# Three subtractions of a gated-mix kernel moved from VectorE to GpSimd, and ScalarE's copies moved behind the value rows

## The chip, the cores and the metric

The kernel runs on one core of a Trainium2 chip. TensorE (PE) multiplies, VectorE (DVE), ScalarE (ACT) and GpSimd (POOL) work element by element, and SyncE (SP) issues the DMAs. Each engine takes its instructions in the order in which the program lists them; semaphores make an instruction wait for another engine. The metric is the device time of one execution in microseconds (us), lower is better.

## The reference

For 2048 tokens of 576 features, the result mixes an attention with a compressive memory (32 heads of 18, four segments of 512 tokens) and a GEGLU feed-forward layer of 4608 hidden features:

```python
x = A_x                                              # (1, 2048, 576)
g = _sigmoid((x * gate_w).sum(-1, keepdims=True))
a = _A_ref(x, wq, wk, wv, wo, beta)                  # segments s = 0..3, memory M, z
b = (_gelu(x @ w_gate) * (x @ w_up)) @ w_down
return g * a + (1 - g) * b

# in _A_ref, for each segment s:
p = _softmax(qs @ ks.T * scale + mask);  a_dot = p @ vs
a_mem = (phi(qs) @ M) / (phi(qs) @ z + 1e-6)
o = g * a_mem + (1 - g) * a_dot
M = M + phi(ks).T @ vs;  z = z + phi(ks).sum()
```

## The kernel before

All float32 operands are split into a high and a low float16 word, and a product is the sum of three products of words. The program first projects x to queries, keys and values, one segment of 512 tokens at a time (s = 0 to 3, the first 212 us), and then runs 72 steps of the feed-forward layer with attention heads placed between the products.

The order of the instructions on each engine is that in which the code is written (a manual schedule); no planner reorders them.

A segment s from 1 to 3 begins with four rows of values, q = 0 to 3, of 128 tokens each. In one row, TensorE forms the first half of the values (`vrows(s, q, 0)`), turns the keys of the segment before (`key_rows`, bank G and V), forms the second half (`vrows(s, q, 1)`), reads the memory with the queries (`recall`, two banks "st", line 683), and adds the row of the segment before to the memory (`memorize`, line 737). For these, VectorE writes the low words of the values (`vstage`, line 654) and of the keys (`krow`, line 724), and normalises what was recalled (`put_recall`: lines 694 to 705, of which line 703 multiplies two 128x32 tensors in SBUF and line 705 reads the banks "st" for the last time). A bank of PSUM can be written again only when these have read it. After the rows come nine projections (`project`, line 447).

The feed-forward products are formed by a scheme with fewer products that needs sums of quarters of x. `load_sums(p)` brings two segments into `acc`; `form_sums(p, i, half, by)` makes the i-th of three sums (line 482, a float32 subtraction of 128x1024, both inputs in SBUF), its high word on ScalarE (line 484) and its low word on VectorE (line 486, again two inputs in SBUF); `last_sum` makes the fourth (its subtraction, line 491, always ran on GpSimd). For p = 0 this lies in the rows of s = 2, for p = 1 the subtractions lie in the rows of s = 3 and the words in its projections.

GpSimd otherwise sets the last column of a `vstage` buffer at each row's beginning (line 647, a memset that waits until `memorize` has let go of an older buffer). In s = 3 it scales the first weights (`scales_out`, lines 275 to 278, then `scale_g`, line 303).

Of the kernel before, what the change touches and what calls it, by code (L numbers as in the profile page):

```python
# [45 lines left out]
def kernel(ctx: ExitStack, tc: tile.TileContext, xs, wqk, wv, wo, wgu, wd, beta, out):  # L46
    nc = tc.nc
    pe, act, dve, pool, sp = nc.tensor, nc.scalar, nc.vector, nc.gpsimd, nc.sync
# [19 lines left out]
    def flat(ap):  # L68
        return ap.rearrange("p a b -> p (a b)") if len(ap.shape) == 3 else ap
# [102 lines left out]
    def add_squares(c, ks, to=0, by=pool):  # L172

        for k in ks:
            a, b = (x_sq[c][:, i * L : (i + 1) * L] for i in (to, k))
            by.tensor_tensor(a, a, b, OP.add)
# [42 lines left out]
    def rescale(c):  # L219

        a, b = slice(c, c + 1), slice(c + 1, c + 2)
        v = rescales[c] = cst.tile([P, 1], F32, name="xr", tag="xr", bufs=2)
        dve.tensor_scalar(v, xsc[:, b], xis[:, a], None, OP.mult)
        for t in (xsc, xis):
            dve.tensor_copy(t[:, a], t[:, b])

    def rescale_words(c):
        dve.tensor_scalar(flat(x16[c]), flat(x16[c]), rescales.pop(c), None, OP.mult)
# [235 lines left out]
    def load_sums(p):  # L464
        c = 2 * p
        r = sums_x[p] = {}
        o = (1 + 4 * p) * 2 * L
        for i in range(2):
            for h in range(2):
                r[h + 1, i + 1] = kept["words"][:, o + 2 * h * L : o + 2 * (h + 1) * L]  # L470
            sp.dma_start(kept["words"][:, o : o + 4 * L], flat(xs[c + i, :, 0:4]))
            o += 4 * L

    def form_sums(p, i, half, by=dve):

        r, sc = sums_x[p], xsc[:, 2 * p : 2 * p + 1]
        t = kept["xt"][p] if half >= 0 else None
        k, o, a, b = ((0, (1, 1), (1, 2), (1, 1)), (2, (1, 2), (2, 2), (1, 2)), (1, (2, 2), (2, 2), (1, 1)))[i]
        if t is not None:
            hi, lo = (flat(t[:, 4 * k + j : 4 * k + j + 2]) for j in (0, 2))  # L480
        if half <= 0:
            by.tensor_tensor(r[o], r[a], r[b], OP.subtract)
        if half == 0 or half == 2:
            act.activation(hi, r[o], AF.Copy, scale=sc)
        if half == 1:
            dve.scalar_tensor_tensor(lo, r[o], sc, hi, OP.mult, OP.subtract)
# [39 lines left out]
    with tc.tile_pool(name="prj", bufs=2, side="right", reuse_waits="tile") as pp:  # L526
# [56 lines left out]
        def finish_later():  # L583
            while later:
                later.pop(0)()
# [55 lines left out]
        def put_rows(s, q, b, pv, unit, a):  # L641

            hf, c = divmod(s, 2)
            t = 4 * c + q
            if b == 0:
                st = vst[s, q] = pa.tile([P, H, VC], F16, name="vstage", bufs=6)
                pool.memset(st[:, :, VC - 1 : VC], 1.0)
            st = vst[s, q]
            p3 = pv[:, :NH].rearrange("p (h d) -> p h d", d=DH)
            hs = slice(16 * b, 16 * b + 16)  # L650
            act.activation(st[:, hs, DH : 2 * DH], p3, AF.Copy, scale=unit)

            def rest():
                dve.scalar_tensor_tensor(st[:, hs, 0:DH], p3, unit, st[:, hs, DH : 2 * DH], OP.mult, OP.subtract)
                if b:
                    dve.tensor_scalar(gate[:, 0, 8 * hf + t : 8 * hf + t + 1], pv[:, NH : NH + 1], a, None, OP.mult)
                    sp.dma_start(vps[hf][t * P : (t + 1) * P, :], flat(st))

            later.append(rest)
# [117 lines left out]
        with tc.manual_schedule(engines=ORDERED):  # L777
# [91 lines left out]
            def beside_rows(s, q):  # L869
                if 0 < s < 3 and q == 0:  # L870
                    add_squares(s, range(1, KT))
                if s == 1 and q == 1:
                    add_squares(0, range(1, KT))
                if s == 1 and q == 0:
                    load_sums(0)
                if s == 1 and q == 2:
                    rescale(0)
                    rescale_words(0)
                if s == 2:
                    if q > 1:  # L880
                        form_sums(0, q - 2, 1)
                    if q:
                        form_sums(0, q - 1, 0)
                if s == 3 and q == 0:
                    rescale(2)
                    for i in range(2):
                        squares(0, 1, i, lambda o, r: square_sum(o, r, True))
            def behind_rows(s, q):
                if s == 3:
                    if q == 1:  # L890
                        scales(0)
                        scales_out(0)
                        scale_g(0)
                        scale_g(1)
                    if q < 3:
                        form_sums(1, q, -1, pool if q == 0 else dve)
                    if q == 3:
                        rescale_words(2)
                        high_g(0, 0)
                        low_g(0, 0)  # L900
# [91 lines left out]
            for s in range(4):  # L992
                p = s - 1
                if s:
                    for q in range(4):
                        pv = vrows(s, q, 0)
                        if q == 0:
                            key_scale(p)
                        if done:
                            put_columns(*done)  # L1000
                            done = None
                        finish_later()
                        put_rows(s, q, 0, *pv)
                        if s == 3 and q == 0:
                            norm_x(3, bank("V"))
                        if q:
                            key_rows(p, q - 1)
                        beside_rows(s, q)
                        finish_later()
                        if held:  # L1010
                            held.pop()()
                        behind_rows(s, q)
                        pv = vrows(s, q, 1)
                        put_rows(s, q, 1, *pv)
                        if p >= 1:
                            recall(p, q)
                        if q:
                            memorize(p, q - 1)
                    finish_later()
                    key_rows(p, 3)  # L1020
                for j in range(9):
                    if j == 1 and s:
                        make_gate(s)
                    if s and j == 0:
                        memory_scale(p)
                    if s or j > 1:
                        pr = project(s, j)
                    elif j == 0:
                        prs = project_first()
                        pr = prs[0]  # L1030
                    else:
                        pr = prs[1]
                    if s and j == 0:
                        finish_later()
                        memorize(p, 3)
                    if s == 0 and j in (2, 3, 5, 6):
                        make_qk(j + 2 + (j == 3))
                    if done and (s, j) != (0, 1):
                        for d in done if isinstance(done, list) else [done]:
                            put_columns(*d)  # L1040
                    done = [done, pr] if (s, j) == (0, 1) else pr
                    if s and j == 1:
                        keep_memory(p)
                    if s == 3 and j == 1:

                        first.close()
                        mp2 = stay.enter_context(tc.tile_pool(name="ffn2", bufs=2, reuse_waits="tile"))
                        xt.append(mp2.tile([P, 12, L], F16, name="xt1", bufs=1))
                        home.update(r=mp2)
                    beside_products(s, j)  # L1050
                    finish_later()
                    if (s, j) == (1, 3):
                        make_gate(0)
                    if s == 0 and j >= 6:
                        q = j - 5
                        pv = vrows(0, q, 1)
                        put_rows(0, q, 1, *pv)
                    if s == 3 and j == 6:
                        recall(3, 0, (("dn", 2), ("dn", 2)))
                        recall(3, 1, (("V",), ("pv",)))  # L1060
                    if s == 3 and j == 7:
                        recall(3, 2, (("dn", 2), ("dn", 2)))
# [766 lines left out]
```

## Time and profile before

| | us |
|---|---|
| median of 3 runs | 1555.67 (1555.64 to 1556.55) |
| span of the profiled execution | 1553.8 |
| what lies around the span, by the median | 1.9 |
| PE busy | 1548.4 |
| POOL busy | 1305.8 |
| DVE busy | 1229.3 |
| ACT busy | 1183.7 |

No separate time is given for the profiled execution; the median is 1.9 us above its span, which is taken for what lies around it. Busy time of PE is that of pipelined matmuls with modelled ends, so it is read together with the waits. A segment's place in the span: the rows of s = 2 lie from 99 to 122 us, those of s = 3 from 151 to 175 us.

### The profile page before, as it was taken

The numbers are of one execution on the slowest core, as the hardware profiler recorded it, in microseconds if no ns is written. First come the engines' busy times: TensorE is split into PE (matmuls) and PEld (weight loads), VectorE is DVE, ScalarE is ACT, GpSimd is POOL, SyncE is SP. The second block draws the span as 40 slices with busy tenths as digits, with TensorE's granted clock in tenths as the row PEclk, the third lists the DMA queues.
The fourth block names the chain that finished last, engine by engine and source line by source line (L and its number), as shares of the span: only waits on it lengthen the run. The fifth ranks groups of instructions, "written<-read, shape, count | busy, mean of one in ns | idle before, by whom it ended". The sixth has DMA issues, their size and how long they took to land.

```text
span 1553.8 us, 33925 instructions
## 1 busy us (share of the span) xinstructions
PE 1548.4 (100%) x12195; PEld 955.7 (62%) x12196; DVE 1229.3 (79%) x3198; ACT 1183.7 (76%) x2037; POOL 1305.8 (84%) x1313
## 2 busy tenths in 40 slices
PE   9999999999999999999999999999999999999999
PEld 5665655666666566666666665666666666666577
DVE  6788976778878887878788887878787878887665
ACT  7567544888888888888888888888888888876421
POOL 3544778899898999989899989898999989899597
PEclk9999999999999999999999999999999999999999
DMA  7533341667768687778777878878687878774654
GB/s 254 195 127 125 132 150 34 122 126 140 133 131 141 130 144 130 144 126 137 132 136 126 140 139 136 135 140 151 127 138 133 144 128 141 130 136 99 120 118 138
DMA packets 472601, 210.14 MB, mean 135 GB/s; under 512 B 427632, under 2 KB 437360, under 8 KB 471920
## 3 DMA queue, kind: packets, MB, share of 16 engines
q1 hardware_dynamic: 472432, 207.97, 67.6%
q8 instruction: 96, 1.57, 0.4%
q14 instruction: 73, 0.60, 0.1%
HBM read 92.03 MB, written 27.26 MB: 77 GB/s over the span
## 4 chain that ended last, share of the span: by engine, by line
PE 94%; POOL 3%; ACT 2%; DVE 1%; issue 1%; POOLq 0%
PE dn L1228 27%; PE U L1268 22%; PE V L1268 12%; PE pv L1183 4%; PE G L385 3%; PE st L447 3%; PE dn L454 2%; PE U L1275 2%; PE dn L385 1%; PE U L447 1%; PE V L1280 1%; PE G L1280 1%; PE st L1137 1%; PE G L447 1%; PE st L1669 1%; PE V L1275 1%
## 5 line engine op out<-in xcount | busy, mean ns | idle before, releaser
L1228 PE MATMUL dn<-paird,hh 128*128 128x288 f16 x3396 | 476.5, 286 | 0.2
L1164 POOL TENSOR_TENSOR pf<-pf,ph 128x512 f16<-128x512 f32 (+1 forms) x256 | 359.2, 1403 | 94.6 <-ACT ph L1163 83.6
L1228 PEld LDWEIGHTS <-hh 128*128 128x128 f16 x3456 | 332.2, 98 | 139.1 <-issue 18.1
L1268 PEld LDWEIGHTS <-pairg 128*128 128x128 f16 x2616 | 244.0, 98 | 254.8 <-issue 18.3
L1236 DVE SCALAR_TENSOR_TENSOR acc<-dn,ev,acc 128x288 f32<-128x288 f32 x534 | 274.4, 515 | 51.4 <-PE dn L1228 42.9
L1153 ACT ACTIVATE pf<-pf,mb,esc 128x512 f32<-128x512 f32 (+3 forms) x512 | 293.0, 642 | 5.2
L1268 PE MATMUL U<-xt,pairg 128*128 128x512 f16 x864 | 209.9, 379 | 0.2 <-DVE gl L1459 0.2
L1268 PE MATMUL U<-x,pairg 128*128 128x512 f16 x840 | 204.1, 379 | 0.0
L426 POOL TENSOR_TENSOR pairg<-raw,pairg 128x640 f16<-128x640 f32 (+2 forms) x144 | 176.2, 1239 | 3.0 <-ACT pairg L418 1.5
L1163 ACT ACTIVATE ph<-pf 128x512 f16<-128x512 f32 (+1 forms) x256 | 172.4, 720 | 0.0
L1255 POOL TENSOR_TENSOR hh<-gl,hh 128x512 f16<-128x512 f32 x144 | 164.4, 1163 | 7.5 <-ACT hh L1254 7.5
L1140 DVE CUSTOM_DVE_ANT_0 pf<-st,mask 128x512 f32<-128x512 f32 (+1 forms) x256 | 157.2, 614 | 0.0
L418 ACT ACTIVATE pairg<-raw 128x640 f16<-128x640 f32 (+2 forms) x144 | 89.3, 647 | 56.6 <-POOL raw L410 36.2
L1258 ACT ACTIVATE gl<-gl,sc 128x512 f32<-128x512 f32 x144 | 97.2, 716 | 40.7 <-DVE gl L1505 30.1
L303 POOL TENSOR_SCALAR raw<-raw,sc 128x640 f32<-128x640 f32 x72 | 118.7, 1663 | 0.0
L1459 DVE COPY gl<-U 128x512 f32<-128x512 f32 x72 | 49.8, 692 | 85.4 <-PE U L1268 74.9
L1150 ACT ACTIVATE mb<-mx,esc 128x4 f32<-128x4 f32 x128 | 37.5, 293 | 103.4 <-DVE mx L1140 103.4
L1140 DVE CUSTOM_DVE_ANT_0 pf<-dn,mask 128x256 f32<-128x256 f32 (+1 forms) x192 | 67.2, 375 | 55.3 <-PE dn L1137 55.3
L1268 PE MATMUL V<-xt,pairg 128*128 128x512 f16 x432 | 105.7, 381 | 0.0
L1268 PE MATMUL V<-x,pairg 128*128 128x512 f16 x432 | 104.8, 378 | 0.0
L1254 ACT ACTIVATE hh<-gl 128x512 f16<-128x512 f32 x144 | 82.6, 616 | 16.0 <-DVE gl L1250 15.8
L1183 PEld LDWEIGHTS <-pt 128*128 128x128 f16 x2560 | 83.4, 96 | 12.3
(354 smaller groups left out, 2971.1 us busy)
## 6 DMA issues: line engine op xcount, KB each, us to landing
raw<-in_wgu_dram SPq DMA_DIRECT2D x36, 640.0 KB
rawd<-in_wd_dram SPq DMA_DIRECT2D x36, 288.0 KB
qk<-stage SPq DMA_DIRECT2D x36, 256.0 KB
qt<-qk SPq DMA_DIRECT2D x128, 72.0 KB
kt<-qk SPq DMA_DIRECT2D x128, 72.0 KB
vp<-vstage SPq DMA_DIRECT2D x16, 296.0 KB
vt<-vp SPq DMA_DIRECT2D x16, 296.0 KB
qt<-qk SPq DMA_DIRECT2D x128, 36.0 KB
```

What stands on the lines that cost most here:

```text
L303: pool.tensor_scalar(r, r, scl[f // 2][0][:, 0:1], None, OP.mult)
L426: pool.tensor_tensor(spot(f, *p, 1), raw_g[f][:, p[0] : p[1]], spot(f, *p, 0), OP.subtract)
L1140: dve.tensor_tensor_reduce(prob[a][:, COL[qi] : COL[qi] + (qi + 1) * P], out[qi], mask[:, L - (qi + 1) * P :], 1.0, -3e38, OP.add, OP.max, ...
L1153: act.activation(r, r, AF.Exp, bias=b[:, qi : qi + 1], scale=esc[:, 0, c : c + 1])
L1163: act.activation(h[:, cols], p[:, cols], AF.Copy)
L1164: pool.tensor_tensor(p.bitcast(F16)[:, cols], p[:, cols], h[:, cols], OP.subtract)
L1183: pe.matmul(ov, pr[:, 10 * i + COL[qi] // P + kb], v[:, 4 * e + kb, c0 : c0 + VC], start=kb == 0 and i == 0, stop=kb == qi and i == 1)
L1228: pe.matmul(o[:, :NH], hh[:, a, q * P : (q + 1) * P], w[:, b, n * NH : (n + 1) * NH], start=i == 0, stop=i == 5)
L1236: dve.scalar_tensor_tensor(av, o[:, :NH], ev, av, OP.mult, OP.add)
L1255: pool.tensor_tensor(hh[:, 1], t, hh[:, 0], OP.subtract)
L1258: act.activation(t, o, AF.Gelu_apprx_tanh, scale=scl[f // 2][0][:, 2 + c : 3 + c])
L1268: pe.matmul(o, w[:, i, (a + k) * P : (a + k + 1) * P], x[:, b + k], start=start and k == 0 and i == 0 and b == h, stop=k == 1 and i == 1, ...
```

## The change

In s = 2 the subtractions for i = 1 and i = 2 (rows q = 2 and q = 3) go from VectorE to GpSimd; that for i = 0 (row q = 1) stays on VectorE. The ScalarE copies (line 484) of all three go from before the row's second half to behind it. In s = 3 the subtraction for i = 1 (row q = 1) goes to GpSimd, ahead of `scales(0)`; it stood behind that on VectorE. That for i = 0 was on GpSimd and that for i = 2 stays on VectorE.

```diff
                     if q > 1:
                         form_sums(0, q - 2, 1)
                     if q:
-                        form_sums(0, q - 1, 0)
+                        form_sums(0, q - 1, -1, pool if q > 1 else dve)
...
                 if s == 3:
+                    if q < 2:
+                        form_sums(1, q, -1, pool)
                     if q == 1:
                         scales(0)
                         scales_out(0)
                         scale_g(0)
                         scale_g(1)
-                    if q < 3:
-                        form_sums(1, q, -1, pool if q == 0 else dve)
+                    if q == 2:
+                        form_sums(1, q, -1)
...
                         pv = vrows(s, q, 1)
                         put_rows(s, q, 1, *pv)
+                        if s == 2 and q:
+                            form_sums(0, q - 1, 2)
```

On GpSimd in the rows of s = 2 (the memsets are those of the rows q = 1, 2 and 3; line 176 sums squares of x, line 491 is `last_sum`, line 629 belongs to the projections):

```order
 L647 MEMSET vstage 128x32
 L176 TENSOR_TENSOR pairg_960<-pairg_960 128x512 x4
-L647 MEMSET vstage 128x32 x3
+L647 MEMSET vstage 128x32 x2
+L482 TENSOR_TENSOR acc<-acc 128x1024
+L647 MEMSET vstage 128x32
+L482 TENSOR_TENSOR acc<-acc 128x1024
 L491 TENSOR_TENSOR acc<-acc 128x1024
 L629 TENSOR_TENSOR phi<-phi,expm 128x512
```

One subtraction now follows the memset of row q = 2, one that of row q = 3, and `last_sum` follows the second directly.

On VectorE in row q = 3 of s = 2 (behind `put_recall` of the row before):

```order
 L705 TENSOR_TENSOR mo<-st,rden 128x180
 L486 SCALAR_TENSOR_TENSOR xt_102<-acc,xsc,xt_102 128x1024
-L482 TENSOR_TENSOR acc<-acc 128x1024
 L654 SCALAR_TENSOR_TENSOR vstage<-dn,vstage 128x16x18
 L724 SCALAR_TENSOR_TENSOR krow_173<-G,kmc,krow_173 128x448
```

The subtraction between the low word of the sum before and the values' low words is gone; the same piece stands in row q = 2.

On GpSimd in row q = 1 of s = 3 (the first subtraction is i = 0, the memset is that of row q = 1):

```order
 L482 TENSOR_TENSOR acc<-acc 128x1024
 L647 MEMSET vstage 128x32
+L482 TENSOR_TENSOR acc<-acc 128x1024
 L275 TENSOR_SCALAR sc<-v 128x2
 L276 TENSOR_SCALAR sc<-xis,v 128x4
```

The second subtraction stands directly behind the memset and ahead of the scales.

## Rows read from the trace of the kernel before

**Rows 1.** Page, part 1: busy us (share of span) xinstructions of each engine.

```profile
PE 1548.4 (100%) x12195; PEld 955.7 (62%) x12196; DVE 1229.3 (79%) x3198; ACT 1183.7 (76%) x2037; POOL 1305.8 (84%) x1313
```

**Rows 2.** Busy time by window: stretch, its us, each engine's busy us, clock, DMA.

```profile
98.00:125.00 27.00, 27.00 (x234) 22.43 (x233) 25.22 (x67) 11.86 (x23) 12.31 (x12) 1.00 0.40 138
150.00:176.00 26.00, 26.00 (x230) 22.08 (x229) 24.06 (x71) 12.74 (x30) 20.16 (x19) 1.00 0.49 165
```

**Rows 3.** Waits of PE from 98 to 250 us: total us, times, longest.

```profile
PE U L1268 <- DVE gl L1459: 0.2, 1, 0.2
```

**Rows 4.** Timeline, DVE, rows of s = 2: start, us, instruction, [idle before].

```profile
108.58 0.46 DVE L654 SCALAR_TENSOR_TENSOR vstage<-dn,vstage 128x288 f16<-128x288 f32 x1 [0.31 <-ACT vstage L651]
...
110.19 0.19 DVE L703 TENSOR_TENSOR rden<-rden,gh 128x32 f32<-128x32 f32 x1
...
113.48 0.45 DVE L654 SCALAR_TENSOR_TENSOR vstage<-dn,vstage 128x288 f16<-128x288 f32 x1
...
115.08 0.46 DVE L654 SCALAR_TENSOR_TENSOR vstage<-dn,vstage 128x288 f16<-128x288 f32 x1 [0.31 <-ACT vstage L651]
...
116.69 0.19 DVE L703 TENSOR_TENSOR rden<-rden,gh 128x32 f32<-128x32 f32 x1
...
119.98 0.45 DVE L654 SCALAR_TENSOR_TENSOR vstage<-dn,vstage 128x288 f16<-128x288 f32 x1
120.35 0.68 DVE L724 SCALAR_TENSOR_TENSOR krow<-G,kmc,krow 128x448 f16<-128x448 f32 x1
```

**Rows 5.** Timeline, POOL: memsets of s = 2, memset and subtraction of s = 3.

```profile
109.81 0.24 POOL L647 MEMSET vstage<- 128x32 f16 x1 [0.33 <-PE pv L737]
115.97 0.24 POOL L647 MEMSET vstage<- 128x32 f16 x1 [5.92 <-PE pv L737]
...
155.46 0.24 POOL L647 MEMSET vstage<- 128x32 f16 x1
155.54 2.35 POOL L482 TENSOR_TENSOR acc<-acc 128x1024 f32<-128x1024 f32 x1
```

**Rows 6.** Timeline: VectorE with two SBUF inputs beside a GpSimd tensor-tensor.

```profile
128.07 0.63 DVE L756 TENSOR_TENSOR bd<-bd,kjunk 128x456 f32<-128x456 f32 x1
...
172.04 3.47 POOL L426 TENSOR_TENSOR pairg<-raw,pairg 128x640 f16<-128x640 f32 x2 [0.69 <-ACT pairg L418]
...
174.89 0.67 DVE L703 TENSOR_TENSOR rden<-rden,gh 128x32 f32<-128x32 f32 x1
...
179.10 2.35 POOL L491 TENSOR_TENSOR acc<-acc 128x1024 f32<-128x1024 f32 x1
...
179.87 2.08 DVE L756 TENSOR_TENSOR bd<-bd,kjunk 128x456 f32<-128x456 f32 x1
...
185.28 1.27 POOL L629 TENSOR_TENSOR phi<-phi,expm 128x512 f32<-128x512 f32 x1 [0.90 <-DVE phi L628]
...
185.80 1.83 DVE L486 SCALAR_TENSOR_TENSOR xt<-acc,xsc,xt 128x1024 f16<-128x1024 f32 x1
```

**Rows 7.** Timeline: VectorE subtractions beside GpSimd instructions with one tensor input.

```profile
161.20 1.26 POOL L275 TENSOR_SCALAR sc<-v 128x2 f32<-128x2 f32 x1 [3.13 <-DVE v L268]
...
165.27 3.91 POOL L303 TENSOR_SCALAR raw<-raw,sc 128x640 f32<-128x640 f32 x2
...
166.22 1.22 DVE L482 TENSOR_TENSOR acc<-acc 128x1024 f32<-128x1024 f32 x1
```

**Rows 8.** Timeline, PE: recall and memorize in row q = 3 of s = 2.

```profile
119.73 1.37 PE L683 MATMUL st<-bd,phi 128*128 128x152 f32 x10
120.94 0.82 PE L737 MATMUL U<-vstage,krow 128*128 128x152 f16 x9
```

**Rows 9.** Timeline, row q = 1 of s = 3: DVE's normalising, PE's next recall.

```profile
158.22 0.19 DVE L703 TENSOR_TENSOR rden<-rden,gh 128x32 f32<-128x32 f32 x1
158.45 0.82 DVE L705 TENSOR_TENSOR mo<-st,rden 128x396 f32<-128x396 f32 x2
...
159.76 1.37 PE L683 MATMUL st<-bd,phi 128*128 128x152 f32 x10
```

## The prediction

> **What bounds the kernel now.** First the page: PE is busy for 1548.4 of 1553.8 us [rows 1]. Then the stretches in which the change lies: in the rows of s = 2 and of s = 3, PE and VectorE are both busy throughout (27.00 and 25.22 of 27 us, 26.00 and 24.06 of 26 us), while GpSimd has 12.31 and 20.16 us of work in them [rows 2]. Then PE's waits from 98 to 250 us: a single one, 0.2 us [rows 3]. So TensorE sets the time, and VectorE runs close behind it without holding it up. Work taken from VectorE shortens nothing here; whatever makes VectorE late by more than its slack becomes a wait of PE, and later work does not give it back, since PE is busy there too.
>
> How small the slack is, two places show. In row q = 3 of s = 2, `memorize` starts at 120.94 with nine products about 0.07 us apart [rows 8]; its third is the first to read the low words of the keys, at 121.08. VectorE writes these from 120.35 to 121.03 [rows 4]: 0.05 us to spare. In row q = 1 of s = 3, `recall` starts at 159.76 into the banks that line 705 has finished reading at 159.27 [rows 9]: 0.49 us to spare.
>
> **What is removed.** Three subtractions leave VectorE, 1.22 us each [rows 7], 3.66 us together. They stood behind work on which PE waits nowhere, so their removal is worth 0 to the time, at the very most the 0.2 us of [rows 3]. The three copies on ScalarE keep their number and size. Ahead of them now stands the copy of the values' second half, for which VectorE waited 0.31 us in row q = 2 and in the one after [rows 4]; these waits go. ScalarE has 11.86 us of work in 27 [rows 2], so the copies are hidden behind the values there; the low word that reads each copy comes a row later. If that cover were gone, VectorE would wait for a copy, less than the 1.22 us of the subtraction it no longer does.
>
> **What is added.** Three subtractions on GpSimd, 2.35 us each by the one that ran there already [rows 5]. GpSimd has idle time for them, but they do not run alone. In the rows, VectorE instructions with two inputs in SBUF stand still while a GpSimd tensor-tensor runs: line 756 takes 0.63 us by itself and 2.08 when it begins 0.77 us after a 128x1024 subtraction of GpSimd, ending 0.50 us behind that one's end (179.10 + 2.35 = 181.45, against 181.95). Line 703 takes 0.19 [rows 4], but 0.67 beside line 426, ending 0.05 us behind it; line 486 takes 1.83 instead of some 1.27 beside line 629, ending 1.08 us behind it [rows 6]. Whoever starts first keeps the other out for its whole length. GpSimd instructions with one tensor input behave otherwise: a subtraction on VectorE at 166.22 ran in its full-speed 1.22 us in the middle of line 303 [rows 7].
>
> The Trainium skill says the same of the first kind (SBUF — State Buffer, section SBUF: two separate sides): the port pair that VectorE and GpSimd share is an exclusive lock held for a whole instruction, and it counts any GpSimd operation that reads SBUF. For line 303 the trace disagrees (1.22 us, no stretch). By the rule and by the rows of the first kind the sum is the one below; by the row of the second kind it would be zero. The new instructions are tensor-tensor, of the very shape of the 179.10 row, so I take the first.
>
> *Row q = 2 of s = 2.* GpSimd starts 0.08 us after its memset begins (155.46 to 155.54), hence at 109.81 + 0.08 = 109.89, and ends at 112.24 [rows 5]. Line 703 moves up from 110.19 by the vanished wait of 0.31 (0.38, since successive instructions overlap by some 0.07): 109.80 to 109.88 [rows 4]. It starts first, by 0.08 us at best. Line 486 then waits for GpSimd and ends at 112.24 + 1.08 = 113.32; the next values' low word begins 0.08 earlier, 113.24, instead of 113.48. Price: 0. Had GpSimd been first, line 703 would end at 112.29, lines 705 (0.82, [rows 9]) and 486 (1.27) follow, and VectorE would be 0.8 us late; PE's `memorize` would then wait some 0.4 us.
>
> *Row q = 3 of s = 2.* From 113.24 the second half's low word comes 1.22 later (113.48 to 115.08 less the wait of 0.38), 114.46, and line 703 another 1.61 later (115.08 to 116.69): 116.07. GpSimd's memset is released by PE at 115.97, so its subtraction starts at 116.05 and ends at 118.40 [rows 4, 5]. GpSimd is ahead by 0.02 us, which is as good as a tie; each extra wait on VectorE makes GpSimd the first, and I take it so. Then line 703 ends at 118.45, lines 705 take 0.8, and line 486 comes at 119.22, but `last_sum`, which no longer waits for VectorE, has started on GpSimd at 118.48 and runs to 120.83. Line 486 ends at 121.91, the values' low word starts at 121.83 instead of 119.98, so the low words of the keys are ready at 122.88 instead of 121.03 and PE's third product waits from 121.08: **1.8 us**. Queued behind on PE are the next keys' turning and the projections, which only move with it. Were VectorE first, line 486 would end at 119.50 and nothing would be late: 0.
>
> *Row q = 1 of s = 3.* The subtraction follows the one of 155.54 (ends 157.89), so it runs from 157.97 to 160.32; its data had to be there for the first already, which also reads both segments. Line 703 comes at 158.22, a quarter of a microsecond too late, and ends at 160.37; the first instruction of line 705 starts 0.03 later and takes 0.57 of the pair's 0.82, so the bank is free at about 161.0, against `recall` at 159.76: **1.25 us** [rows 5, 9]. Bounds: 0 if line 703 came first, 1.5 if PE waits for both of line 705. The keys' low words then end at 162.2, before `memorize` wants them at 162.4. `scales_out` on GpSimd starts late by about 2 us, but its first instruction took 1.26 us at 161.20, beside the subtraction that leaves [rows 7]; most of that comes back, so GpSimd is 1 to 1.25 us late while PE is 1.25 us late. No further price.
>
> **Sum.** 1555.67 + 0 + 1.8 + 1.25 = 1558.7 us. It is made on the profiled execution's 1553.8 us (1556.85 after), and the 1.9 us around the span are taken as unchanged; the median of the runs is this execution's time in that sense.
>
> **The rivals.**
> - *VectorE wins the tie in row q = 3.* For it: 0.02 us decides, and a single shorter wait on VectorE turns it. Against it: VectorE's start is a sum of five steps, and delays are likelier than gains. Only s = 3 costs: 1555.67 + 1.25 = 1556.9.
> - *GpSimd wins in row q = 2 as well.* For it: VectorE's lead is at most 0.08 us. Then 0.4 more in that row and as much as 2.1 in the next, since VectorE enters it later: 1555.67 + 0.4 + 1.8 + 1.25 = 1559.1, at the bounds of each 1559.6.
> - *GpSimd's idle time hides the subtractions.* For it: 12.31 of 27 us busy, and line 303 beside line 482. Against it: [rows 6]. VectorE gains 3.66 us of slack, PE has nothing to give: 1555.5 to 1555.9.
> - *The other side, faster.* If PE's products in the rows were paced by VectorE without a recorded wait, a share of 3.66 us would come back. It decides from 3.1 us, nearly all of it; PE has 27.00 busy in 27 us against it. 1552.
>
> **Chances and range.** The forecast 0.45 (1558.7, by itself 1558.2 to 1559.1); VectorE wins the tie 0.30 (1556.9); GpSimd wins twice 0.12 (1559.1 to 1559.6); hidden 0.11; faster 0.02. A range of 1556.5 to 1559.5 leaves out the last two and a little above. Within 0.2% (3.1 us, about what a measurement of this kernel can tell from no change) lie the tie's other end, the hidden case and rather more than half of the forecast, whose 3.05 us stand just under that line: 0.67. Slower by more: the rest of the forecast and most of the double loss, 0.31. Faster: 0.02.
>
> **What would show it.** Right: line 703 at 2 us instead of 0.19 in rows q = 3 of s = 2 and q = 1 of s = 3, a wait of PE at `memorize` near 121.1 and at `recall` near 159.8 plus what came before, line 486 stretched in both rows of s = 2, and no other new wait of PE up to 250 us. Wrong: line 703 at 0.19 in s = 3 although a subtraction runs on GpSimd (the exclusion does not hold), `last_sum` standing behind line 486 (the tie fell the other way), a wait of ScalarE or PE for a copy of line 484, or a new wait later than 180 us, where I expect the shift to pass through unchanged.

## The result, and the profile after

In 21 runs of each kernel on the same chip the changed kernel takes 1558.78 us (median; 1557.29 to 1559.91), the kernel before 1556.55 (1555.35 to 1558.04). The ratio is 1.0014, 95% interval 1.0007 to 1.0020: slower by 2.2 us (1.1 to 3.1), which is 0.14%. The prediction's sum was 1558.7, 3.05 us above its starting point of 1555.67. That start is the median of three runs and lies 0.88 below the median of the 21; the step is 0.8 larger than the measured one. That the sum meets 1558.78 almost exactly is therefore luck: the two errors cancel. The direction is right; the size needs the traces, for the profiled execution holds only one of the two waits of PE that the sum is made of.

The page of the kernel after, part 1, busy us (share of the span) and instructions:

```profile
PE 1548.0 (99%) x12195; PEld 954.8 (61%) x12196; DVE 1231.5 (79%) x3195; ACT 1183.7 (76%) x2037; POOL 1311.9 (84%) x1316
```

Beside [rows 1], three instructions have gone from VectorE to GpSimd, and yet VectorE is 2.2 us busier: 3.66 us of subtractions left it, and stretched instructions put more than that back. Busy time does not tell work from standing still.

The waits of PE in the whole span of the kernel after (engine, bank and line, what it waits for; us in total, times, longest):

```profile
PE U L737 <- DVE krow L724: 1.7, 1, 1.7
PE dn L674 <- DMA acc<-in_wv_dram: 1.2, 2, 1.0
...
PE U L1272 <- DVE gl L1463: 0.2, 1, 0.2
```

Between 98 and 250 us [rows 3] has one wait of 0.2 us, at 248 us in the feed-forward steps, which is still there (last row); here the first row is new. It is `memorize` waiting for the low words of the keys, the wait that the prediction puts at row q = 3 of s = 2. A wait of `recall` for line 705 is not among the rows. Line 674 waits for the first loads (at 4 to 8 us), and PE is 0.50 us later than in the kernel before already at 42 us (line 457 at 42.17 against 41.67). No change in the rows can cause that.

Timeline of TensorE after, row q = 3 of s = 2, and the first `recall` in the rows of s = 3:

```profile
120.23 1.37 PE L683 MATMUL st<-bd,phi 128*128 128x152 f32 x10
121.44 0.30 PE L737 MATMUL U<-vstage,krow 128*128 128x152 f16 x2
123.44 0.68 PE L737 MATMUL U<-vstage,krow 128*128 128x152 f16 x7 [1.70 <-DVE krow L724]
...
156.91 1.37 PE L683 MATMUL st<-bd,phi 128*128 128x152 f32 x10
```

In [rows 8] the nine products run on without a break from 120.94. Here two run at 121.44 (0.50 later), and the third starts at 123.44 instead of 0.14 behind, 121.58: 1.86 us lost. By the starts of its products PE stands 0.50 us behind the kernel before ahead of this place (120.23 against 119.73) and 2.37 behind at the first `recall` of s = 3 (156.91 against 154.54), and the spans differ by 2.4 (1556.2 against 1553.8).

VectorE after, rows of s = 2, and line 703 in row q = 1 of s = 3 (timeline):

```profile
110.43 0.19 DVE L703 TENSOR_TENSOR rden<-rden,gh 128x32 f32<-128x32 f32 x1
...
111.40 2.53 DVE L486 SCALAR_TENSOR_TENSOR xt<-acc,xsc,xt 128x1024 f16<-128x1024 f32 x1
...
116.65 2.31 DVE L703 TENSOR_TENSOR rden<-rden,gh 128x32 f32<-128x32 f32 x1
...
119.73 2.69 DVE L486 SCALAR_TENSOR_TENSOR xt<-acc,xsc,xt 128x1024 f16<-128x1024 f32 x1
122.35 0.45 DVE L654 SCALAR_TENSOR_TENSOR vstage<-dn,vstage 128x288 f16<-128x288 f32 x1
122.72 0.67 DVE L724 SCALAR_TENSOR_TENSOR krow<-G,kmc,krow 128x448 f16<-128x448 f32 x1
...
160.16 0.19 DVE L703 TENSOR_TENSOR rden<-rden,gh 128x32 f32<-128x32 f32 x1
```

GpSimd after, the same places (timeline):

```profile
110.43 2.41 POOL L482 TENSOR_TENSOR acc<-acc 128x1024 f32<-128x1024 f32 x1
...
116.57 2.35 POOL L482 TENSOR_TENSOR acc<-acc 128x1024 f32<-128x1024 f32 x1
118.99 2.36 POOL L491 TENSOR_TENSOR acc<-acc 128x1024 f32<-128x1024 f32 x1
...
160.35 2.35 POOL L482 TENSOR_TENSOR acc<-acc 128x1024 f32<-128x1024 f32 x1
```

Read the two side by side. In row q = 2 both start at 110.43; line 703 keeps its 0.19 of [rows 4], and only line 486 behind it is held, to 113.93. In row q = 3 GpSimd starts at 116.57, 0.08 us ahead of line 703, which then takes 2.31 us and ends at 118.96. Line 486 comes at 119.73, when `last_sum` has run since 118.99, and ends at 122.42. Behind it come lines 654 and 724, 2.37 us later than in [rows 4], and these end at 123.39, just ahead of PE's 123.44. In s = 3 line 703 is ahead, 160.16 against 160.35, and takes 0.19: in this execution there is nothing to wait for.

### The profile page after: what moved, and what is told of

It reads as the page before. It is cut to its first block, busy times and chain, and to the rows that moved or that the text cites. A ratio compares the mean times of both kernels' runs of the same rounds, so it can differ in the third digit from the quotient of the medians.

```text
span 1556.2 us, 33926 instructions
## 1 busy us (share of the span) xinstructions
PE 1548.0 (99%) x12195; PEld 954.8 (61%) x12196; DVE 1231.5 (79%) x3195; ACT 1183.7 (76%) x2037; POOL 1311.9 (84%) x1316
## 4 chain that ended last, share of the span: by engine, by line
PE 92%; POOL 3%; ACT 2%; DVE 2%; issue 1%; DMA 0%; SPq 0%; POOLq 0%
PE dn L1232 27%; PE U L1272 22%; PE V L1272 12%; PE pv L1187 4%; PE G L385 3%; PE st L447 3%; PE U L1279 2%; PE dn L454 2%; PE dn L385 1%; PE U L447 1%; PE V L1284 1%; PE G L1284 1%; PE st L1141 1%; PE G L447 1%; PE st L1673 1%; PE V L1279 1%
```

## The experiments

What was open after this: whether the loss in s = 3 is there at all, what decides between VectorE and GpSimd, and whether exclusion is the cause of each wait, rather than the copies or the added work as such. The medians below are each beside runs of the kernel before on the same chip, whose own medians are 1555.9 (first four kernels) and 1556.07 (the next two); each stands as a ratio with its 95% interval. One interval is 2.6 to 3.1 us wide, as much as what is looked for, so the waits in the traces tell more than the times.

**The part in s = 3 alone** (`e1_s3_only`): the kernel before with this edit.

```diff
                 if s == 3:
+                    if q < 2:
+                        form_sums(1, q, -1, pool)
                     if q == 1:
                         scales(0)
...
-                    if q < 3:
-                        form_sums(1, q, -1, pool if q == 0 else dve)
+                    if q == 2:
+                        form_sums(1, q, -1)
```

> The kernel before with the part in s = 3 alone (subtraction i = 1 on GpSimd ahead of the scales). Theory (exclusive port pair, and the order of arrival decides): without the wait in s = 2, line 703 in row q = 1 comes about 0.25 us behind the start of GpSimd's second subtraction, takes about 2.1 us instead of 0.19, and PE waits 1.2 to 1.3 us at recall (line 683) near 160 us: +1.25 us. Rival 1 (the weights' DMA lands at another time in each execution and not because of the wait in s = 2): line 703 comes first here as well, no wait of PE, 0 us. Rival 2 (GpSimd is never in the way in s = 3): line 703 at 0.19 even while the subtraction runs, 0 us.

Measured: 1557.33 us, ratio 1.0008 (0.9999 to 1.0016). The wait of PE that is new:

```profile
PE st L683 <- DVE mo L705: 1.2, 1, 1.2
```

By the starts of its products PE loses 1.38 us there. VectorE, then GpSimd, in row q = 1 of s = 3 (timelines of this kernel):

```profile
158.44 2.00 DVE L703 TENSOR_TENSOR rden<-rden,gh 128x32 f32<-128x32 f32 x1
160.48 0.82 DVE L705 TENSOR_TENSOR mo<-st,rden 128x396 f32<-128x396 f32 x2
```

```profile
158.05 2.35 POOL L482 TENSOR_TENSOR acc<-acc 128x1024 f32<-128x1024 f32 x1
```

GpSimd is ahead by 0.39 us, and line 703 ends at 160.44, as the subtraction ends (160.40). So the wait that the profile after lacks does exist.

**The part in s = 2 alone** (`e2_s2_only`): the changed kernel with the edit above undone.

> The changed kernel with s = 3 as it was before. Theory: all of the loss lies in row q = 3 of s = 2: line 703 at about 2.3 us, line 486 at 2.7, one wait of PE at line 737 for line 724 of 1.7 us by the list of waits, 1.9 us by the starts of the products, and none in s = 3: +1.9 us. Rival (the part in s = 3 bears some of the loss): less than 1.5 us.

Measured: 1557.86 us, ratio 1.0011 (1.0002 to 1.0020). The same wait of 1.7 us at `memorize` as after (1.86 by the starts), and none at `recall`. In row q = 2 line 703 and the subtraction start in the same hundredth of a microsecond, 109.88, and line 703 takes 0.19; in row q = 3 the subtraction starts at 116.01, line 703 at 116.09, and it takes 2.31. So the part in s = 2 costs its wait also without the part in s = 3, and all of it lies in row q = 3.

**The copies alone** (`e3_copies_only`): the kernel before, with the subtractions left where they were and only the copies moved.

```diff
                     if q:
-                        form_sums(0, q - 1, 0)
+                        form_sums(0, q - 1, -1)
...
                         put_rows(s, q, 1, *pv)
+                        if s == 2 and q:
+                            form_sums(0, q - 1, 2)
```

> The kernel before with ScalarE's three copies moved behind the values' second half, all subtractions on VectorE where they were. Theory: the wait of 0.31 us of VectorE's line 654 for ScalarE is gone in rows q = 1 and 2, PE waits nowhere new, 0 us. Rival (the moved copies delay something that PE needs): a wait of PE between 107 and 125 us of 0.3 us or more.

Measured: 1556.36 us, ratio 1.0001 (0.9992 to 1.0010), and no new wait of PE from 100 to 200 us. Line 703 of row q = 3 starts at 115.69, only 0.13 us behind GpSimd's memset at 115.56. So the moved copies cost nothing themselves; with the vanished waits they bring VectorE close to the tie.

**The inverse in PSUM** (`e4_inverse_in_psum`): the changed kernel, with what line 703 multiplies taken from spare columns of the bank "st", so that only one of its two inputs lies in SBUF. The subtractions on GpSimd stay as they are.

```diff
-            dn = pp.tile([P, H], F32, name="den", bufs=2)
+            dn, inv = nb[:, 400 : 400 + H], nb[:, 440 : 440 + H]
...
-            dve.reciprocal(rd, dn)
-            dve.tensor_tensor(rd, rd, gh[:, 0], OP.mult)
+            dve.reciprocal(inv, dn)
+            dve.tensor_tensor(rd, inv, gh[:, 0], OP.mult)
```

> The changed kernel, with the 32 denominators and their inverses of put_recall kept in spare columns of the bank st, so that line 703 has one input in SBUF and one in PSUM; all else as changed. Theory (two SBUF inputs make it wait): line 703 takes about 0.2 us while GpSimd subtracts, line 486 comes ahead of last_sum and is stretched only to the end of the subtraction, VectorE is no later than before, and PE waits neither at line 737 nor at line 683: back to the kernel before, 0 us. Rival (VectorE is held up by GpSimd's use of SBUF whatever the inputs are): line 703 still above 2 us and PE's wait of 1.9 us stays.

Measured: 1556.16 us, ratio 1.0001 (0.9992 to 1.0010). Both waits are gone from PE's list, and one of 0.2 us stands there instead, at 202.9 us, behind the rows:

```profile
PE dn L683 <- DVE mo L705: 0.2, 1, 0.2
```

VectorE, then GpSimd, in row q = 3 of s = 2 of this kernel (timelines):

```profile
116.35 0.19 DVE L703 TENSOR_TENSOR rden<-st,gh 128x32 f32<-128x32 f32 x1
116.58 0.82 DVE L705 TENSOR_TENSOR mo<-st,rden 128x396 f32<-128x396 f32 x2
117.32 2.28 DVE L486 SCALAR_TENSOR_TENSOR xt<-acc,xsc,xt 128x1024 f16<-128x1024 f32 x1
```

```profile
116.16 2.36 POOL L482 TENSOR_TENSOR acc<-acc 128x1024 f32<-128x1024 f32 x1
118.59 3.22 POOL L491 TENSOR_TENSOR acc<-acc 128x1024 f32<-128x1024 f32 x1
```

Line 703 starts behind the subtraction (by 0.19 us, in the lost row of the profile after by 0.08), and takes 0.19 instead of 2.31. Line 486, still with two inputs in SBUF, waits for GpSimd's end (118.52) and ends at 119.60. It has got its place before `last_sum`, which starts 0.07 us after the subtraction's end and takes 3.22 us instead of 2.36: now GpSimd is the one that waits, and nobody waits for it.

In row q = 1 of s = 3 GpSimd is ahead by 0.53 us, and line 703 is not held there either:

```profile
158.60 0.19 DVE L703 TENSOR_TENSOR rden<-st,gh 128x32 f32<-128x32 f32 x1
```

```profile
158.07 2.36 POOL L482 TENSOR_TENSOR acc<-acc 128x1024 f32<-128x1024 f32 x1
```

PE's `recall` follows 5.22 us behind the first one of s = 3, as in the kernel before. This is the experiment that shows the cause of both waits: the same GpSimd work at the same place costs nothing once line 703 is not kept out.

**The last subtraction of s = 2 back on VectorE** (`e5_last_row_on_dve`): the changed kernel with that of row q = 2 on GpSimd alone.

```diff
-                        form_sums(0, q - 1, -1, pool if q > 1 else dve)
+                        form_sums(0, q - 1, -1, pool if q == 2 else dve)
```

> The changed kernel with the subtraction of row q = 3 in s = 2 (i = 2) back on VectorE; that of q = 2 stays on GpSimd, and so does that of s = 3. Theory (the two waits of PE exclude each other: the one in s = 2 moves PE and VectorE against the landing of the first weights and lets line 703 come first in s = 3): line 703 at 0.19 in both rows of s = 2, no wait of PE there, line 703 at about 2.0 in row q = 1 of s = 3 and a wait of PE of 1.2 us (1.4 by the starts) at line 683 near 160 us: +1.4 us. Rival (something else in the changed kernel's s = 2, as the copies or the subtraction of q = 2, brings line 703 ahead in s = 3): no wait of PE at all, 0 us.

Measured: 1557.30 us, ratio 1.0007 (0.9997 to 1.0017). No wait of PE in s = 2: line 703 of row q = 3 takes 0.19, line 486 1.28. In s = 3 GpSimd starts at 157.76 and line 703 at 158.19 for 1.97 us, and PE waits 1.2 us (1.36 by the starts). The subtraction of row q = 2 on GpSimd is free, then, and the whole loss in s = 2 belongs to row q = 3.

**The fourth sum later** (`e6_last_sum_late`): the changed kernel with `last_sum` two places later, so that line 486 does not find GpSimd busy.

```diff
                     if j == 0:
                         form_sums(0, 2, 1)
+                    if j == 2:
                         last_sum(0, 0)
-                    if j == 1:
+                    if j == 3:
                         last_sum(0, 1)
```

> The changed kernel with last_sum's subtraction and words (lines 491 to 497 for p = 0) two projections later, so that in row q = 3 of s = 2 no GpSimd instruction follows the subtraction. Theory (two exclusions in a row, each paid by VectorE): line 703 still takes 2.3 us, line 486 only 1.28, VectorE comes 1.4 us earlier than in the changed kernel and PE's wait at line 737 shrinks from 1.9 to 0.4 to 0.5 us by the starts; in s = 3 the order is open, since the wait of s = 2 is then nearly as short as the lead of 0.25 us that GpSimd has without it: +0.4 or +1.4 to 1.8 us. Rival (line 703 alone makes up the loss): PE's wait stays at 1.9 us.

Measured: 1557.14 us, ratio 1.0010 (1.0000 to 1.0019). The waits of PE:

```profile
PE dn L456 <- DVE x L215: 0.7, 1, 0.7
...
PE U L737 <- DVE krow L724: 0.3, 1, 0.3
```

Line 703 still takes 2.31 us (from 116.03), but line 486 takes 1.28 (from 119.11), and the wait at `memorize` shrinks from 1.7 to 0.3 (from 1.86 to 0.44 by the starts). So line 703's block by itself makes some 0.4 us of the loss, and the second one, of line 486 by `last_sum`, the other 1.4. The time is not back, for the moved words make VectorE late at another place: line 497, now at 139.15, waits 0.94 us for its high word, VectorE has hardly any idle time from there to line 215 at 152.04, and PE loses 0.9 us waiting for that one (first row). This was not expected. In s = 3 line 703 came first here (159.93 against 160.15), since GpSimd's chain was late: its first subtraction starts 1.93 us behind the first `recall` of s = 3, in the others 1.0 to 1.1.

**The changed kernel three times more** (`e7_changed_again_a`, `e8_changed_again_b`, `e9_changed_again_c`), with no edit, one profile each: what does s = 3 do from one execution to another?

> The changed kernel once more, for the order of arrival in s = 3. Measured so far: ScalarE's square of the first weights, which waits for their DMA, starts from 0.39 us before to 0.56 us after PE's first recall of s = 3 in the executions seen, and in the run with the part in s = 2 alone it moved along with PE. Theory A (PE's wait in s = 2 always lets VectorE be first in s = 3): one wait of PE, 1.9 us at line 737, none at line 683, square at least 0.3 us before the first recall. Theory B (the landing differs from one execution to the next and decides): the square at 0 or later in some execution, then line 703 at about 2 us in s = 3 too and a second wait of PE of about 1.3 us.

> As the run before it: theory A, no wait of PE in s = 3 in any execution of the changed kernel; theory B, a wait of about 1.3 us at line 683 in those in which the square of the first weights starts at the first recall or later.

> As the two before it: theory A, no wait of PE in s = 3; theory B, one of about 1.3 us where the square of the first weights starts at the first recall or later.

Measured: 1558.69, 1559.74 and 1559.05 us, beside one run of the kernel before, 1555.57; spans 1556.9, 1557.7 and 1557.3. All three have both waits, 1.86 us by the starts at `memorize` and 1.37, 1.50 and 1.36 at `recall`. So theory A is refuted, and with it that of `e5_last_row_on_dve`, that the two waits exclude each other. TensorE, VectorE, GpSimd and ScalarE in s = 3 of the first of them (timelines, in this order):

```profile
156.09 1.37 PE L683 MATMUL st<-bd,phi 128*128 128x152 f32 x10
...
162.69 1.01 PE L683 MATMUL st<-bd,phi 128*128 128x152 f32 x6 [1.21 <-DVE mo L705]
```

```profile
159.96 1.98 DVE L703 TENSOR_TENSOR rden<-rden,gh 128x32 f32<-128x32 f32 x1
161.97 0.82 DVE L705 TENSOR_TENSOR mo<-st,rden 128x396 f32<-128x396 f32 x2
```

```profile
159.54 2.35 POOL L482 TENSOR_TENSOR acc<-acc 128x1024 f32<-128x1024 f32 x1
```

```profile
156.32 0.74 ACT L556 ACTIVATE kjunk<-raw 128x640 bf16<-128x640 f32 x1 [0.55 <-DMA raw<-in_wgu_dram]
...
157.92 0.41 ACT L651 ACTIVATE vstage<-dn 128x288 f16<-128x288 f32 x1
```

ScalarE in the profile after, at the same place:

```profile
156.52 0.74 ACT L556 ACTIVATE kjunk<-raw 128x640 bf16<-128x640 f32 x1 [0.28 <-DMA raw<-in_wgu_dram]
...
158.12 0.41 ACT L651 ACTIVATE vstage<-dn 128x288 f16<-128x288 f32 x1
```

Count from the first `recall` of s = 3, 156.91 in the profile after and 156.09 here. GpSimd's second subtraction starts at +3.44 and +3.45: the same. Line 703 starts at +3.25 and +3.87. What differs ahead of it is ScalarE: its square (line 556) waits for the first weights to land and starts at −0.39 and +0.23, the copy of the values' second half (line 651) behind it at +1.21 and +1.83, and for this copy VectorE waits. In the ten profiles with line 703 as it was, line 703 starts 3.62 to 3.64 us behind the square. Over all eleven profiles the square starts between −0.39 and +0.56 (at +0.56, in `e6_last_sum_late`, no wait for the transfer stands ahead of it), and the one at −0.39 is the only one of the four of the changed kernel without the second wait.

In all profiles but that of `e6_last_sum_late`, SyncE issues the load of these weights at the same place, 5.24 to 5.25 us ahead of that `recall`. The profile after, then the first repeat (timelines):

```profile
151.66 0.34 SPq L235 DMA_DIRECT2D raw<-in_wgu_dram  x1
```

```profile
150.84 0.35 SPq L235 DMA_DIRECT2D raw<-in_wgu_dram  x1
```

So not the issue differs but the landing, and by these traces it decides who is first: with GpSimd at +3.45 and line 703 at 3.64 behind the square, VectorE is ahead when the square starts some 0.2 us or more before the `recall` (an estimate from these two). No run moves the landing by itself, so this much is read from the order in the traces; why it lands differently stays open.

## Why the prediction was right

*What is removed: right.* 3.66 us left VectorE, and no wait of PE became shorter; the moved copies alone change nothing (1.0001).

*The exclusion: right, and shown.* A VectorE instruction with two inputs in SBUF stands still behind a GpSimd tensor-tensor until that one ends, and with one input moved to PSUM it does not (2.31 against 0.19 us). The rule that the prediction took from the Trainium skill (SBUF — State Buffer, section SBUF: two separate sides) agrees for these instructions, down to the operand in PSUM, since it names two SBUF inputs; for line 303 it does not (last section).

*Row q = 2 of s = 2, price 0: right.* VectorE's lead was put at 0.08 us at best; it was 0.00 in the profile after and in each of the three repeats, and line 703 went first every time. Which of the two a lead of 0.00 would let through the prediction could not tell, so that part was luck. Line 486 was stretched, to 2.53 us, and PE did not wait.

*Row q = 3 of s = 2, 1.8 us: right.* It was called as good as a tie and taken for GpSimd, because a wait more on VectorE would decide it; the lead came out at 0.08 us instead of 0.02. That is what happened: the subtraction of row q = 2 ended 2.53 us behind its memset's start (110.31 to 112.84) instead of the 2.43 of the prediction, and line 486 and VectorE came 0.1 later by it. Line 703 ends with the subtraction, `last_sum` follows and holds line 486, and the third product waits: 1.86 us in every profile of the changed kernel. The rival that VectorE wins this tie happened in none.

*Row q = 1 of s = 3, 1.25 us: the mechanism was right, the size a little low, and one assumption was not seen.* Where the wait occurs it is 1.36 to 1.50 us. Mis-sized was the way back from line 705 to PE: in the first of the repeats its first instruction ends about 162.54 (161.97 and the 0.57 of the prediction), and `recall` starts at 162.69, 0.15 us later; the prediction let PE start as the bank came free. The `recall` itself then takes 0.08 longer (its ten products 1.45 instead of 1.37), which the prediction left out. Not seen was that "GpSimd first, by a quarter of a microsecond" holds for one landing of a transfer; the lead was 0.39 to 0.58 us in the five profiles with this wait, and −0.19 in the profile after.

*The sum: inside its range, a little small for both waits and too large for the median.* From the first rows of s = 2 to the third `recall` of s = 3, PE loses 1.86 us in the profile after and 3.3, 3.4 and 3.3 in the repeats, which have both waits; 3.05 was predicted. The spans of the repeats, 3.1 to 3.9 us above the 1553.8 of before, hold besides what the first loads of each execution did (PE comes to the rows 0.3 us earlier to 0.4 us later than before). The median of 21 runs is only 2.2 above, as would follow if it mixes executions with one wait and with both. How many had which is not shown, since only one of the 21 has a profile; their spans would fit, with nine at 1555.3 to 1556.4, among them the profiled one with one wait (1556.2), and twelve at 1556.6 to 1557.9, where the repeats lie. No gain came later: the shift passes through 180 to 250 us unchanged, to 0.1 us, and GpSimd's later start in s = 3 causes no wait.

No kernel here beats the one before, whose PE waits nowhere in the rows; the version with the inverse in PSUM keeps the moved subtractions at no measurable price.

## What to carry to other kernels

Before work goes to an idle GpSimd, look which VectorE instructions will meet it: a tensor-tensor of 2.35 us there can stop a 0.19 us instruction with two inputs in SBUF for its whole length, and what then counts is who waits for the short one. Put one of its inputs into PSUM, or place the GpSimd work where long and uncritical VectorE work stands, as in row q = 2 here. Where two starts lie within a few tenths of a microsecond, price both orders, and look for a transfer ahead of either that lands at different times in different executions.

## What the runs showed of the hardware that was not expected

Line 303, the GpSimd instruction with one tensor input, excludes too, but only at its beginning. VectorE after, beside line 303, whose four instructions take 1.87 us each (timelines):

```profile
164.67 0.46 DVE L703 TENSOR_TENSOR rden<-rden,gh 128x32 f32<-128x32 f32 x1
...
168.18 1.73 DVE L482 TENSOR_TENSOR acc<-acc 128x1024 f32<-128x1024 f32 x1
```

```profile
164.30 7.48 POOL L303 TENSOR_SCALAR raw<-raw,sc 128x640 f32<-128x640 f32 x4
```

Line 703 starts 0.37 us behind an instruction of line 303 and takes 0.27 longer than its 0.19; line 482 starts 0.14 us behind the third of them (164.30 + 2 x 1.87 = 168.04) and takes 0.51 longer than its 1.22. Both come out at 0.64 to 0.65 us from the start of GpSimd's instruction, after which VectorE runs freely beside it. The subtraction of [rows 7] came 0.95 us behind and ran at full speed; the prediction had read it as no exclusion at all. The trace of before already had a row against that reading (VectorE, then GpSimd):

```profile
163.88 0.35 DVE L703 TENSOR_TENSOR rden<-rden,gh 128x32 f32<-128x32 f32 x1
```

```profile
163.39 1.90 POOL L303 TENSOR_SCALAR raw<-raw,sc 128x640 f32<-128x640 f32 x1
```

Here line 703 starts 0.49 behind and takes 0.16 longer, which gives 0.65 again. With the inverse in PSUM it starts 0.52 behind (163.26 against 162.74) and takes its 0.19, ending 0.71 behind. In the ten profiles with the line as it was, line 703 starts 0.37 to 0.49 us behind that instruction of line 303 and ends 0.83 to 0.84 us behind its start. For other GpSimd instructions with one tensor input no row here shows it.

And where both engines start in the same hundredth of a microsecond (row q = 2 of s = 2 in all seven profiles that have this subtraction and line 703 as it was, as 110.43 after, 109.88 in the part in s = 2 alone, 109.62 in the first repeat), VectorE went first each time. GpSimd's recorded start is not one held up by line 703: it comes 0.12 us after its memset's start there (110.31 after), and so it does with the inverse in PSUM (109.91 and 110.03), where line 703 comes 0.16 later and excludes nobody. Nor is line 703's start held up by GpSimd: with the copies alone, and no subtraction on GpSimd there, it too comes 0.12 us after the memset's start (109.40 and 109.52). So as far as GpSimd's recorded starts can be trusted these are true ties, and GpSimd paid for them with 2.41 us instead of 2.37. A lead of 0.08 us was enough for GpSimd in row q = 3.
